# Attention with a memory, mixed with an S4 convolution, on one core: another stored order of the same 1,802 steps

## The chip, the core and the metric

The kernel runs on 1 core of one Trainium2 chip. The metric is device time in microseconds of one execution. The engines are named as in the profile: PE (TensorE) multiplies matrices, DVE (VectorE) and ACT (ScalarE) do the elementwise work, POOL (GpSimd) does next to nothing here, and SP (SyncE) issues all the DMA transfers.

## The reference

The input x has 2048 tokens of width 512. Two branches are computed from it and mixed per token:

```python
g = sigmoid((x * gate_w).sum(-1))            # one gate per token
out = g * A(x) + (1 - g) * B(x)

# A: 32 heads of width 16, tokens in 4 segments of 512
for s in range(4):
    a_dot = softmax(qs @ ks.T / 4 + causal_mask) @ vs      # inside the segment
    a_mem = (phi(qs) @ M) / (phi(qs) @ z + 1e-6)           # from the segments before
    o[s]  = sigmoid(beta) * a_mem + (1 - sigmoid(beta)) * a_dot
    M, z  = M + phi(ks).T @ vs, z + phi(ks).sum()          # phi(t) = t + 1 if t > 0 else exp(t)
A = o @ wo

# B: a long convolution per channel, 512 channels, 128 states
K[d, l] = Re( sum_n C[d,n] * exp(dt[d] * A[d,n] * l) * dt[d] * B[d,n] )
B = irfft(rfft(x padded) * rfft(K padded)) + x * Dskip
```

## The kernel before

The work is cut into 1,802 small steps, each an instruction or a short run of instructions on one engine, or one DMA transfer. They carry names:

- `pk`, `pq`, `tok` (s, hg): projections of segment s and group hg of 8 heads to keys, queries and values. Each is 4 matmuls and an eviction from PSUM.
- `sc`, `mk`, `pv`, `nrm` (s, hg, kind): scores, an exponential of 128x2048 on ACT (line 1067), a mask on DVE (line 1079) for the later groups, the product with the values and its division (lines 1041 and 1042). There are 80 such exponentials.
- `st`, `mem`, `os`, `oT`: the memory state, its use, the sum of both parts (line 1130) and the transposed heads.
- `pow` and `pwc` (h, k): the powers of the convolution's decay by squaring, for two halves h of the channels. Each power is copied into a second place by a DMA from SBUF to SBUF of 64 KB. `tab` (c): products of the powers (lines 1180, 1183 and 1187 on DVE) into tables for each of 4 quarters of the channels; `lag` (c): the convolution kernel from the tables.
- `xl1`: the first level of a Fourier transform of x, written to a scratch tensor in DRAM, `scr_Z`.
- For each half (a, b) of the channels and t from 0 to 15: `Zx`, `CT`, `CD` load a piece of `scr_Z` and of the constants `c_DNM` (128x768 and 128x1280); `X` is the second level of the transform, whose result is copied to the other half of the partitions by two DMAs of 64 KB; `K` transforms the convolution kernel; `Y` (line 1298 on DVE) multiplies both, and `V` transforms back and is written by a DMA to where `fir` collects it.
- `fir`, `Cl`, `fin`: the last level with the token gate, out to DRAM and back, and the output projection with the gated add (lines 1365, 1368 and 1369).
- `gate`: the factors from beta (lines 857 to 863); `xTl`: x loaded and transposed (line 700 for segments 1 to 3).

Nothing in these steps is tied to a place in the program. A string, `ORDER`, lists all of them in one order; `build_kernel` reads it, and `replay` gives each engine its steps in that order. A word of the string is the step's number, then `a` or `v` where the step is an eviction that either ACT or DVE may do, then, after slashes, the number of the buffer for each tile that is taken there:

```python
        for w in ORDER.split():
            w = w.split("/")
            order.append((int(w[0].rstrip("av")), "ACT" if w[0][-1] == "a" else "DVE", [int(v) for v in w[1:]]))
        S.replay(order)
        S.emit()
```

So the string decides four things: the order on each engine and on SP's queue, which of ACT and DVE evicts, which buffer and which PSUM bank a tile gets, and with these what each instruction waits for. `emit` puts the waits in. An engine runs its steps strictly in its order: a step that waits holds up all behind it, and a DMA whose data is not ready holds up the transfers behind it on SP.

Of the kernel before, what the change touches and what calls it, by code (L numbers as in the profile page):

```python
# [369 lines left out]
15/0 8/1 0/0 9/4 25/6/0 14/0 26v 31/0/0 57/0 32 41/0 34/1 42/5 1202/1 6/0 10/0 35/2 33/10 36/3 60/5 37 38 39 40/3 58/7 61v/0 47/0 43/11 23/0 11/1 48/1  # L370
16/0 49/4 51/0 50 59a 44 1220/5/0 64/7 12/2 62/3 45 1218/0 1219a 63 3/0 1210/3/1 18/0 1/0 65v/8 74/2 46 76/0 1221a 75 27/1/1 204/0/2 22/0 201/2/1/0
28v 53/0 88/6 13/3 20/0 86/1 87 1211a 195/0 29/1/0 77v/5 176/1 100/2 52/11 19 98/0 4/0 99 205a 209/0/0 56/0 1222 54/2 30v 202a 203 110/3 112/3 66
220/0/0 17 111 67 113v/1 221 181/4 89v/0 182/0 192/0 124/0 122/1 123 101v/7 125v/2 222 179/3 102 1223/0 213/1 207/2 210a 126 778/0 114 136/2 177/1 90
229/0/1 134/2 1208/3 137v/4 103 214v 230 249/0/0/1 215/1/1/0 55 208a 231 135 196 115 1209a 240/0/2 178/0 180 91 24/0 241 250a 197/0 146/2 216 78 148/3
1236/3/0 252/0/1 147 1237a 70/1 184/1 1212 211/2 242 161v/3 206 982v/0 217 253a 1226/3/1 986 1234/1 224/0/3 149v/6 198/0 79 987/1 68/2 251 988 978v/0
979v 254/0/0/1 212a 980v 1235a 225 127 7/0 293/2/0 981v 162 223/1 160/4 69 226 236/0/0 379/1 158/2 163 294a 993/0 255 992 138 183 159 237 994 218 227
228 232 290/2/2/0 170v/9 256 150 1238 999/0 1224/0 983 984/1 233/0 998 171 1227a 238 985 139 1205/3/0 1225a 291a 270/0/3 271 1206a 235/2 219/0/0
1203/3 234/0 370/0 989 272 257 1000 1228 1204a 80/0 82/6 239 151 995 261/0/1 1001 262 263 172 243 996/0 244 5/0 1002/1 258 1239/1/1 245/2 1241/3 997
292 193 265/0/2 246 1240a 1207 1004 266 1005/0 1229/1/0 1231/2 1242a 264/3 267 1243 277/0/1 194 259/0 278 185 1006 1003 1213/0/1 1232a 1230a 329/1/1/2
279 1214a 281/0/0 330a 1215/2 1244/0 282 990/0 1013 1233 268 269 1216a 991 283 81 276/0 1250/1/0 273 1007 332/2/1 1014/1 1008/0 304/0/3 333a 1015 305  # L380
1009 1016 1251a 280 1017/0 306 1217 1260/1/1 1011/1 284 1262/2 1261a 285 286/3 300/0/0 274/0 301 1010 1263a 1265/1 1018 371/1/0/1 302 334/2/0/0 335
316/0/2 1012 317 372a 92/2 275/1 1023/1/0 1019/3 1024 287 1020 1021 336 1025 94/0 318 93 1264 104/0 337 1027/0 1028 1022v 309/0/1 310 1036a/0 1038v/0
331 1266/2/1 1042 1026a 1043/1 106/2 1267a 107v/0 1268/3 1034v 311 386/1 1044 105 303/2 1269v 1049/0 116/2 307 308 1048 71v/1 312 1037v 1029a 315/3
320/0/0 321 1050 387a 313/1 1055/0 1040/1 247/0 1035a 2/0 322 1252/1 1039 314/0 1270 319 1278/2/1 341/0/1 117/0 342 323 1253a 324 118 1279a 248v/0 343
1254 1041 95v/5 1276/0 374/2/0 83v/7 1054 350/0/0 72 1277a 1045 325/3 295/1/1/1 128/0 73 351 96 1056 326 344/0 1052/1 375a 288/3 352 1245/2/0 345/0/2
346 1057 296 289v 1280 119v/2 1246a 1051 1247/3 429/2/2 347 129/1 130 297 568/0 373 361/0/1 1053 1046/0 362 140/0 430a 1248a 142/2 1058/1 348 141
1257/1/1 349 1255/2 353 382/3 363 1258a 1060 357/0/2 358 356/1 1047 354/0 1061/0 108 383a 120 359 384/3 393/0/0 1059 1062 394 97 1256a 1249 154/3 84
385a 1070/1 355/1 1069 1281/0/0 395 380/2 360 298 1064/0 364 381a 1071 397/0/2 1063 1259 398 131v/3 1072 1067/1 1282a 399 1066 299/0 1283/2 1271/3/1
132 1284a 1272a 409/0/3 1033/0 1068 109 410 1273/2 426/3/1/0 1065 1073/1 365 1030 366/0 1031 85 1032 338 411 413/0/1 414 1074 1285 1274a 367 427a
152/0 396/2 1079/3/0 428 1075/1 1287/0 1076 1077 339 1286/1 415 1080 153 143v/4 1275 1083/0 1084 578/0 155v/6 1081 199 1092v/0 402/0/0 1078a 1090v  # L390
1299/0 186/1 121 1300/1 400 403 166/0 1085a 187/0 1096/0 1091v 1082a 474/0/2/1 133 164/3 156 1093v 1094v/0 1314/1 401 165 1099/1 1301/0 1098 1095 404
523/1/1 457/0/2 458 1088 1100 524v 167a/8 368/3 405 168 1087 144 173v/9 408/1 475a 459 412 1302/0/0 1097 416 417 441/0/0 1288/2 1089 369v 442 406/0
1105/0 1102/1 418/1 388/3/0/0 200 376/0 1303a 1086 407/1 434/0/1/1 1306/2/1 443 1104 419 445/0/1 435 1307a 1106 174 169 1289/1/1 1290a 1101 1111/0 446
1110 436 627/2/0/2 1305 1293/0/0 447 260 437 1112 389 1103 327/1 1304 1294a 450/0/3 145 451 1292 1340/0 378/0 1108/0 444/0 1308/1 1291 328a 1313/0 452
157 390 1309/1/0 1113 1310a 628a 1107 1295/0 175 477/3/0 1312/0 448 476 449 1114/1 1119 461/0/0 462 1296/1/1 520/2/1/0 478a 1339/1 1315/3/0 1109
1327/2 1325/1 340 463 1316a 1297a 453 503/0/1 1116 504 1311/0 1317 1117/0 391 521a 1318 377 505 1345/3/1 454/2 456/1 1118 455/0 1319/2/0 1115 496/0/3
1328/0/2 1346a 497 1320a 460 1329a 464 1366/1 1125 420/1/0/0 1326/1 1321/0 498 1126/1 1365/0 1322/0/0 433/0 1330 421 1323a 1338/0 1120/0 422 1127 423
507/0/2 508 1332/0/0 509 1122 465 392/2/1 431/1 1331 502/3 1298 1128 506 1379/2 1121 1352/1 1341/7/0 1353/0 438 1333a 1129/1 1334/0 1342a 1344 572/4/2
424/7 510 432 511 1343 482/0/1/0 573a 1123/0 1335/4/1 425a/0 1351/1 581/5 512/0 1130 1336a 468/3/1/0 585/4 1124 513/1 582a 1135/5/0 439 574/0 479/1
469 1136 1139/3 586a 1347/0 1140 470 522 483 1131/2 1137 1132 1133 471 1146v/0 1141a 1354/3/1 1149v 1138a 1324 487/0/0 484 1148v 466/0 1150v/0 1134a  # L400
488 1348/2/0 1358/0/1 1147a 1355a 1364/0 576/0 489 1152/1 1371/3/0 491/0/1 629 1151 1349a 467 1153 1357 1154 492 1155/1 1157 485 569/1/2/1 1359a 1372a
472/0 1356 1367/2/0 528/3/0/1 1391/1 493 1156 535/0/2 481/1 1163 1160 1161/0 570v 536 1162 490/1 1368a 494 1360/1 1337 529 537 473a 480 530 579/2
1378/0 1167/0 495 571 1350 1164/1 1361/3/1 499 1166 544/0/0 580a 1369 545 1362a 1370 1377/1 500/0 1168 501 1397/0/1 514/1/5/0 1144 1373/1 1405/0
1392/1 1374/1/0 546 1398a 539/0/1 1390/0 540 1375a 1169 1380/0/0 630/1/0 515 525/1 1381a 1165 516 1404/1 1384/0/0 517 538/2 1418/2 531 541 1393/3/1
1385a 1175 1383 551/0/2 1158/1 1172 1159 1173/0 1382 1376 1176/1 1394a 552 542 486/0 636/3/1/0 543 1363 553 547 1386/0 532 555/0/1 556 631a 1387/1/0
# [1055 lines left out]
```

## Time and profile before

| | us |
|---|---|
| median of 3 runs | 287.19 (286.94 to 290.25) |
| profiled execution | 287.07 |
| its span | 285.3 |
| DVE busy | 265.6 (93%) |
| ACT busy | 261.4 (92%) |
| PE busy | 248.9 (87%) |

The span runs from the first to the last instruction; the execution's own time holds 1.8 us around it. A row of the profile names the engine, the line, the operation, the tensors by name, and at its end in brackets the idle time ahead of it on its engine, with what ended that. Most PSUM evictions pass through one helper, so they carry its lines 226 (ACT) and 227 (DVE); matmuls carry line 663 and plain DMAs line 222.

### The profile page before, as it was taken

The numbers are of one execution on the slowest core, as the hardware profiler recorded it, in microseconds if no ns is written. First come the engines' busy times: TensorE is split into PE (matmuls) and PEld (weight loads), VectorE is DVE, ScalarE is ACT, GpSimd is POOL, SyncE is SP. The second block draws the span as 40 slices with busy tenths as digits, with TensorE's granted clock in tenths as the row PEclk, the third lists the DMA queues.
The fourth block names the chain that finished last, engine by engine and source line by source line (L and its number), as shares of the span: only waits on it lengthen the run. The fifth ranks groups of instructions, "written<-read, shape, count | busy, mean of one in ns | idle before, by whom it ended". The sixth has DMA issues, their size and how long they took to land.

```text
span 285.3 us, 9041 instructions
## 1 busy us (share of the span) xinstructions
PE 248.9 (87%) x3741; PEld 170.4 (60%) x3776; DVE 265.6 (93%) x634; ACT 261.4 (92%) x314; POOL 5.9 (2%) x9
## 2 busy tenths in 40 slices
PE   2767778788687999999999899999989999999995
PEld 1423444465344756777767477876766676889552
DVE  1999999999999999999999999996889999999795
ACT  2999999999999999989999999999878999998832
POOL 0003100000001000000001000000000000000000
PEclk9999997999999999999999999999999999999999
DMA  6969364402825727653656576787667876356966
GB/s 179 212 209 169 97 155 149 149 7 84 122 88 169 181 58 208 186 165 87 177 174 194 137 219 181 194 242 200 192 199 210 258 209 190 77 146 175 264 175 203
DMA packets 61211, 47.71 MB, mean 167 GB/s; under 512 B 23921, under 2 KB 57074, under 8 KB 61170
## 3 DMA queue, kind: packets, MB, share of 16 engines
q1 hardware_dynamic: 61170, 47.13, 60.1%
q8 instruction: 30, 0.49, 0.8%
q14 instruction: 11, 0.09, 0.1%
HBM read 26.79 MB, written 8.39 MB: 123 GB/s over the span
## 4 chain that ended last, share of the span: by engine, by line
PE 35%; DVE 33%; ACT 26%; issue 2%; DMA 2%; SPq 0%; DVEq 0%
PE psum L663 34%; ACT sb L1067 16%; ACT sb L226 8%; DVE sb L1180 5%; DVE sb L1187 5%; DVE sb L1183 5%; DVE sb L227 3%; DVE sb L794 2%; DVE sb L787 2%; DVE sb L786 2%; DMA sb<-sb 1%; DVE sb L1042 1%; DMA sb<-in_B_A_im_dram 1%; ACT sb L940 1%; DVE sb L795 1%
## 5 line engine op out<-in xcount | busy, mean ns | idle before, releaser
L663 PE MATMUL psum<-sb 128*128 128x17 bf16 (+12 forms) x3605 | 241.3, 231 | 26.8 <-ACT sb L1067 14.3
L663 PEld LDWEIGHTS psum<-sb 128*128 128x128 bf16 (+4 forms) x3640 | 161.3, 99 | 100.9 <-ACT sb L1067 27.5
L1067 ACT ACTIVATE sb<-psum 128x2048 bf16<-128x2048 f32 x80 | 152.1, 1901 | 4.7 <-PE psum L663 3.8
L226 ACT ACTIVATE sb<-psum 128x512 bf16<-128x512 f32 (+4 forms) x154 | 88.4, 628 | 3.2 <-PE psum L663 2.8
L1180 DVE TENSOR_TENSOR sb<-sb 128x512 bf16<-128x512 bf16 (+3 forms) x48 | 33.0, 697 | 0.0
L1187 DVE TENSOR_TENSOR sb<-sb 128x512 bf16<-128x512 bf16 (+3 forms) x48 | 32.1, 681 | 0.0
L1183 DVE TENSOR_TENSOR sb<-sb 128x512 bf16<-128x512 bf16 (+3 forms) x48 | 31.9, 674 | 0.0
L227 DVE CAST sb<-psum 128x512 bf16<-128x512 f32 (+2 forms) x41 | 27.6, 674 | 3.0 <-PE psum L663 2.8
L1079 DVE TENSOR_TENSOR sb<-sb 128x1024 bf16<-128x1024 bf16 (+1 forms) x40 | 22.4, 569 | 1.3 <-ACT sb L1067 1.2
L1298 DVE TENSOR_TENSOR sb<-sb 128x1024 bf16<-128x1024 bf16 x32 | 21.7, 680 | 1.9 <-DMA sb<-sb 1.8
L1042 DVE TENSOR_TENSOR sb<-psum,sb 128x256 bf16<-128x256 f32 x32 | 13.2, 414 | 0.1
L227 DVE COPY sb<-psum 128x512 bf16<-128x512 bf16 (+2 forms) x15 | 7.2, 480 | 5.7 <-PE psum L730 5.3
L785 ACT ACTIVATE sb<-sb 128x512 f32<-128x512 f32 x18 | 11.8, 656 | 0.0
L1368 ACT ACTIVATE sb<-psum,sb 128x512 bf16<-128x512 f32 x8 | 5.2, 689 | 5.7 <-DMA out_dram<-sb 5.5
L1041 DVE RECIPROCAL sb<-psum 128x16 f32<-128x16 f32 x32 | 7.9, 248 | 1.4 <-PE psum L663 1.3
L912 POOL COPY sb<-sb 128x128 bf16<-128x128 bf16 x4 | 5.5, 1462 | 149.1 <-PE psum L663 124.0
L1121 DVE TENSOR_TENSOR sb<-psum,sb 128x512 bf16<-128x512 f32 x12 | 8.2, 684 | 0.1
L794 DVE CAST sb<-sb 128x512 bf16<-128x512 f32 x19 | 8.0, 434 | 0.0
L996 ACT ACTIVATE sb<-sb 128x512 bf16<-128x512 bf16 x12 | 7.5, 636 | 0.1
L940 ACT ACTIVATE sb<-psum 128x512 bf16<-128x512 bf16 x12 | 7.6, 637 | 0.0
L1337 DVE TENSOR_TENSOR sb<-psum,sb 128x512 bf16<-128x512 f32 x11 | 7.4, 687 | 0.2 <-PE psum L663 0.2
L786 DVE TENSOR_TENSOR sb<-sb 128x256 f32<-128x256 f32 x18 | 7.5, 417 | 0.0
(74 smaller groups left out, 120.7 us busy)
## 6 DMA issues: line engine op xcount, KB each, us to landing
sb<-c_DNM SPq DMA_DIRECT2D x28, 320.0 KB, 3.8
sb<-sb SPq DMA_DIRECT2D x84, 64.0 KB, 2.9
sb<-c_DNM SPq DMA_DIRECT2D x28, 192.0 KB, 3.1
scr_Z<-sb SPq DMA_DIRECT2D x16, 256.0 KB, 2.2
sb<-scr_Z SPq DMA_DIRECT2D x32, 128.0 KB, 3.1
sb<-sb SPq DMA_DIRECT2D x32, 128.0 KB
sb<-in_A_x_dram SPq DMA_DIRECT2D x5, 512.0 KB, 4.8
scr_C<-sb SPq DMA_DIRECT2D x8, 256.0 KB, 2.6
```

Of the source, the lines that this page charges most:

```text
L226: fa = lambda e: e.activation(dst(), src(), ACT.Copy)
L227: fd = lambda e: e.tensor_copy(dst(), src())
L663: mm = lambda e, o_, l, r_, st, sp, **kw: e.matmul(o_, lhsT=l, rhs=r_, start=st, stop=sp, skip_group_check=True, **kw)
L786: op("DVE", ("V1", 256), lambda e, nz=nz, sq=sq: e.tensor_tensor(ap(nz, 0, n=256), ap(sq, 0, n=256), ap(sq, 256, n=256), ALU.subtract), r= ...
L794: "DVE": (("Vs2", 512), lambda e, dst=dst, src=src: e.tensor_copy(dst(), src()))})
L1042: op("DVE", ("V1", 256), lambda e: e.tensor_tensor(ap(o1, gi * 16, [[128, 4], [32, 4], [1, 16]]), ap(T, dims=[[68, 4], [17, 4], [1, 16]]), ...
L1067: o = op("ACT", ("Ax", 2048), lambda e, P=P, pT=pT: e.activation(ap(pT, n=2048), ap(P, n=2048), ACT.Exp, scale=0.25), r=[P], w=[pT])
L1079: op("DVE", ("V2", 128 * nb), lambda e, pT=pT, dims=dims: e.tensor_tensor(ap(pT, dims=dims + [[1, 128]]), ap(pT, dims=dims + [[1, 128]]), ...
L1180: op("DVE", ("V2" if n > 1 else "V1", 256 * n), lambda e: e.tensor_tensor(run(tile, ne, dst, 1), run(tile, ne, src, sstep), fac(cl * 512), ...
L1183: op("DVE", ("V2" if n > 1 else "V1", 256 * n), lambda e: e.tensor_tensor(run(t2, n, 0, 1), run(tile, ne, src, sstep), fac(cl * 512 + 256) ...
L1187: op("DVE", ("V2" if n > 1 else "V1", 256 * n), lambda e: e.tensor_tensor(D_(), D_(), ap(t2, n * 128, [[-n * 128, 2], [2 * n, 64], [1, 2 * ...
L1298: op("DVE", ("V2", 1024), lambda e, Y=Y, XAB=XAB, K3=K3: e.tensor_tensor(ap(Y, dims=[[512, 2], [1, 512]]), ap(XAB, dims=[[512, 2], [1, 512 ...
```

## The change

The string `ORDER` is replaced by another one. The steps, the buffers' sizes and places, the constants and all other code are the same. It was found by a search whose model lets a DMA's landing depend on the packets in which TensorE's instructions are fetched. 42 evictions and copies change engine: 22 go from DVE to ACT and 20 from ACT to DVE. Between them the counts on DVE go from 634 to 632 steps. Every one of the 70 lines of the string changes; the first of them reads

```diff
@@ -367,76 +367,76 @@
 ORDER = """
-15/0 8/1 0/0 9/4 25/6/0 14/0 26v 31/0/0 57/0 32 41/0 34/1 42/5 1202/1 6/0 10/0 35/2 33/10 36/3 60/5 37 38 39 40/3 58/7 61v/0 47/0 43/11 23/0 11/1 48/1
...
+8/3 0/0 15/0 9/0 14/0 23/0 25/0/2 57/1 192/0 26v 1202/0 195/4 31/1/0 193 32 196 6/0 1/0 41/13 34/11 3/0 33/0 36/1 60/0 37 42/2 58/5 38 11/3 10/0 197/0
...
```

What that moves is shown by the instructions as they stand on an engine. On DVE the program begins with the eviction of the first parameters (line 227) and the decay's steps (lines 751 to 757). Before, its first rows were

```order
L227 COPY sb<-psum 128x1024
L752 TENSOR_TENSOR sb<-sb 128x256 x2
L751 TENSOR_TENSOR sb<-sb 128x256
L754 TENSOR_SCALAR sb<-sb 128x256
L755 TENSOR_SCALAR sb<-sb 128x256
```

and now they are

```order
L227 COPY sb<-psum 128x1024
L861 TENSOR_SCALAR sb<-sb 128x32
L858 TENSOR_SCALAR sb<-sb 128x32
L752 TENSOR_TENSOR sb<-sb 128x256 x2
L751 TENSOR_TENSOR sb<-sb 128x256
L754 TENSOR_SCALAR sb<-sb 128x256
L755 TENSOR_SCALAR sb<-sb 128x256
```

Two of the gate's steps (lines 858 and 861) have come in behind the first eviction; on ACT two others (lines 857 and 862) stand likewise around its first exponential, and the load of beta they need is SP's fifth transfer, where it was the ninth.

On SP the load of the constants for step Xb5 is the row `c_DNM 128x768`. Before, it stood behind a load for K (`128x1280`) and the copies of Xb3 and Xa15:

```order
L222 DMA sb<-scr_Z 128x512
L222 DMA sb<-sb 64x512 x2
L222 DMA sb<-c_DNM 128x1280
L222 DMA sb<-sb 64x512 x2
L222 DMA sb<-c_DNM 128x768
```

and now it stands behind a write of V (`8x16x512`) and one copy:

```order
L222 DMA sb<-scr_Z 128x512
L222 DMA sb<-sb 64x512
L222 DMA sb<-sb 8x16x512
L222 DMA sb<-c_DNM 128x768
L222 DMA sb<-sb 64x512
```

It has moved from the 207th to the 200th of SP's 301 transfers.

138 lines of the change are left out of this document (69 added, 69 removed).

## The prediction

> **What bounds the kernel now.** I read the page's busy shares first, then the busy time by stage, then the chain, and last the waits. The page's first part:
>
> ```profile
> PE 248.9 (87%) x3741; PEld 170.4 (60%) x3776; DVE 265.6 (93%) x634; ACT 261.4 (92%) x314; POOL 5.9 (2%) x9
> ```
>
> Three engines are busy for about nine tenths of a span of 285.3 us, so no order of the same steps can be shorter than DVE's 265.6 us plus what cannot be filled at both ends. The stages show where the rest lies (columns: stretch, its length, then busy us and instructions of PE, weight loads, DVE, ACT and POOL, granted clock, DMA share, GB/s):
>
> ```profile
> 0.00:5.30 5.30, 1.09 (x9) 0.87 (x9) 0.02 (x1) 1.28 (x1) 0.40 (x5) 1.00 0.49 127
> 5.30:100.00 94.70, 73.42 (x1129) 43.26 (x1141) 93.98 (x243) 92.94 (x121) 4.73 (x3) 0.98 0.57 141
> 100.00:190.00 90.00, 85.15 (x1376) 62.98 (x1385) 88.53 (x201) 87.70 (x111) 0.73 (x1) 1.00 0.60 169
> 190.00:278.00 88.00, 84.94 (x1218) 61.55 (x1228) 78.83 (x186) 77.51 (x80) 0.00 (x0) 1.00 0.67 193
> 278.00:285.30 7.30, 4.29 (x20) 1.70 (x18) 4.19 (x9) 1.98 (x3) 0.00 (x0) 1.00 0.61 200
> ```
>
> Up to 190 us DVE and ACT are full: DVE idles 0.72 us, then 1.47 us, ACT 1.76 and 2.30 us. From 190 to 278 us TensorE is the full one (idle 3.06 us) while DVE idles 9.17 us and ACT 10.49 us. A stall counts on DVE and ACT in the first 190 us and on TensorE after that. The chain that ended last agrees at its end (start, length, what):
>
> ```profile
> 239.06 17.98 PE psum L663 x281
> 257.28 6.54 PE psum L663 x92
> ...
> 277.97 2.60 PE psum L663 x12
> 280.60 0.70 ACT sb L1368
> 281.66 1.42 DVE sb L1365 x2
> ```
>
> TensorE carries most of the last 40 us, and one copy with two gated adds closes it.
>
> **The change part by part.** All 1,802 steps stay, so the sum has terms only for waits that go, waits that come, and work that changes engine. It is made against the profiled execution, 287.07 us (its span of 285.3 us and 1.8 us around it), 0.12 us under the median of 287.19.
>
> *A, the load for step Xb5.* At 208 us all three engines stand:
>
> ```profile
> 202.76 0.58 SPq L222 DMA_DIRECT2D sb<-c_DNM  x1
> DMA to landing us min/median/max: 5.3/5.3/5.3
> 206.80 0.69 DVE L1079 TENSOR_TENSOR sb<-sb 128x1024 bf16<-128x1024 bf16 x1
> 208.14 2.62 PE L663 MATMUL psum<-sb 128*128 128x256 bf16 x34 [1.26 <-DVE sb L1079]
> 208.56 0.69 DVE L227 CAST sb<-psum 128x512 bf16<-128x512 f32 x1 [1.07 <-PE psum L663]
> 210.16 0.60 ACT L226 ACTIVATE sb<-psum 128x512 bf16<-128x512 f32 x1 [1.35 <-PE psum L663]
> ```
>
> The view names L1079 of DVE, but that ended at 207.49, 0.65 us before TensorE went on, and Xb5 does not read it. What Xb5 reads is the load issued at 202.76: with 5.3 us to land it arrives at 208.06. On SP's queue this load is the `c_DNM 128x768` row. Before, from the write of Vb12 (`8x16x512 x2`, its second) on:
>
> ```order
> L222 DMA sb<-sb 8x16x512 x2
> L222 DMA sb<-scr_Z 128x512
> L222 DMA sb<-sb 64x512 x2
> L222 DMA sb<-c_DNM 128x1280
> L222 DMA sb<-sb 64x512 x2
> L222 DMA sb<-c_DNM 128x768
> ```
>
> and now, from the same write on:
>
> ```order
> L222 DMA sb<-sb 8x16x512
> L222 DMA sb<-scr_Z 128x512
> L222 DMA sb<-sb 64x512
> L222 DMA sb<-sb 8x16x512
> L222 DMA sb<-c_DNM 128x768
> ```
>
> Six transfers stood between, now three, and the load has gone from the 207th to the 200th of SP's 301 transfers; Xb5 keeps its place on TensorE. Three issues of about 0.6 us are 1.8 us, over the 1.26 us wanted. What is late next is TensorE's own work before it, which ended at 206.88. I take **-1.2 us** (0 to -1.35). In the stretch of that load lies one packet of TensorE's instructions:
>
> ```profile
> q8 instruction: 1, 0.02, 1.1%
> ```
>
> The Trainium skill (Runtime: NRT & Kernel Launch, Instruction fetch mechanics) says that an engine's instructions are refilled in blocks of 16 KiB by a DMA queue of its own and that crossing a block is mostly hidden. The 0.02 MB row agrees with the block; by that rule alone nothing is gained from dodging packets and A would come from the earlier issue only, which is one of the rivals' cases below.
>
> *B, the product Yb14.* In the three DVE waits for copies (1.8 us in all) this is the large one:
>
> ```profile
> DVE sb L1298 <- DMA sb<-sb: 1.8, 3, 1.1
> 193.82 0.69 DVE L1298 TENSOR_TENSOR sb<-sb 128x1024 bf16<-128x1024 bf16 x1 [1.13 <-DMA sb<-sb]
> ```
>
> Its last copy is now 16 places ahead of it in the list instead of 10. But it lies in the stage where TensorE is full, so of 1.13 us I count **-0.2** (0 to -1.1).
>
> *C, the end.* The copy of the last transposed heads (step oT3.3) moves ahead of one gated add of 0.75 us, and the sum feeding it no longer queues behind four adds. TensorE runs through there without a gap (2.60 us from 277.97), so the copy is covered: **-0.2** (+0.3 to -0.8, that one add).
>
> *D, work that changes engine.* Of the steps that ran before 190 us, nine go from DVE to ACT and ten the other way. Their prices on DVE (mean ns of one is the last number ahead of the idle part):
>
> ```profile
> L227 DVE CAST sb<-psum 128x512 bf16<-128x512 f32 x38 | 25.8, 681 | 2.7 <-PE psum L663 2.5
> L227 DVE CAST sb<-psum 128x480 bf16<-128x480 f32 x2 | 1.3, 648 | 0.0
> L227 DVE COPY sb<-sb 128x256 bf16<-128x256 bf16 x17 | 3.9, 287 | 0.1
> ```
>
> Five full evictions come (Ka9, Va8, tok2.2, Ka14, Kb14) and three go (Xa9, pk2.2, pq2.2), +1.36; two evictions of table 1's lags come, at most 1.3; one copy of 0.29 more goes than comes, and two casts of the powers go, priced as two of the larger copies at some 0.4 each; the two transposed-head copies cancel. That is +1.3 us on DVE, which idles 2.2 us in that time. After 190 us thirteen steps leave DVE and ten come, where it has room. I take **+0.5** (-0.7 to +1.3).
>
> *E, the gate steps.* They sat in full stretches:
>
> ```profile
> 4.65 0.50 SPq L222 DMA_DIRECT2D sb<-in_A_beta_dram  x1
> 14.48 0.18 DVE L861 TENSOR_SCALAR sb<-sb 128x32 f32<-128x32 bf16 x1
> 18.48 0.23 ACT L857 ACTIVATE sb<-sb 128x32 f32<-128x32 bf16 x1
> 24.12 0.25 ACT L862 ACTIVATE sb<-sb 128x32 f32<-128x32 f32 x1
> ```
>
> Now they run in the first 7 us, where ACT stands until 5.82 us, and beta's load is issued fifth instead of ninth, one issue (0.5 us) ahead of x. That frees some 0.3 us on DVE and 0.5 on ACT, and ACT's first step now waits for beta. Issued near 2.7 us and landing by 5.4, it is hidden behind the wait for the first matmuls; should it take as long as the x loads beside it,
>
> ```profile
> sb<-in_A_x_dram SPq DMA_DIRECT2D x2, 512.0 KB, 4.6
> ```
>
> it lands at 7.3 and everything starts 1.5 us late. **-0.3** (-0.6 to +1.5).
>
> *F, waits that come.* The product Ya9 waited a little before:
>
> ```profile
> 154.75 0.68 DVE L227 CAST sb<-psum 128x512 bf16<-128x512 f32 x1
> sb<-sb SPq DMA_DIRECT2D x2, 64.0 KB, 3.3
> 159.11 0.69 DVE L1298 TENSOR_TENSOR sb<-sb 128x1024 bf16<-128x1024 bf16 x1 [0.36 <-DMA sb<-sb]
> ```
>
> On DVE, before, from that CAST (Xa9) to Ya9 (L1298):
>
> ```order
> L227 CAST sb<-psum 128x512
> L1183 TENSOR_TENSOR sb<-sb 128x512
> L1041 RECIPROCAL sb<-psum 128x16
> L1187 TENSOR_TENSOR sb<-sb 128x128x16
> L970 TENSOR_TENSOR sb<-sb 128x272
> L1187 TENSOR_TENSOR sb<-sb 128x128x4
> L1180 TENSOR_TENSOR sb<-sb 128x128x4
> L227 CAST sb<-psum 128x512
> L1298 TENSOR_TENSOR sb<-sb 128x1024
> ```
>
> and now, where Xa9 is copied by ACT about beside the first of these rows:
>
> ```order
> L1187 TENSOR_TENSOR sb<-sb 128x128x4
> L227 CAST sb<-psum 128x32x16
> L1183 TENSOR_TENSOR sb<-sb 128x512
> L1079 TENSOR_TENSOR sb<-sb 128x4x128
> L1298 TENSOR_TENSOR sb<-sb 128x1024
> ```
>
> Seven instructions and 3.7 us lay between; now four, about 1.9 us at 0.4 to 0.7 each, against copies that need 3.3 us and a second issue. Ya9 may stand for up to 2 us, with DVE's table steps and TensorE's Va9 behind it. DVE may also run late against ACT there, which would hide it. **+0.6** (0 to +2.0).
>
> The sum is -1.2 - 0.2 - 0.2 + 0.5 - 0.3 + 0.6 = -0.8 us, so **286.3 us**. With all low ends it is 287.07 - 4.55 = 282.5, with all high ends 287.07 + 5.1 = 292.2.
>
> **The rivals.** *The waits only move.* In so full a queue the earlier load lands as late, or Xb5's wait reappears at another load: A and B are 0, the sum is +0.6, about 287.7. For it speaks that SP's queue still holds the same 301 transfers at a DMA share of 0.67; against it that A's load is ahead of three whole transfers.
>
> *Much more is gained.* TensorE's waits for ACT's exponentials shrink:
>
> ```profile
> PE psum L663 <- ACT sb L1067: 14.3, 27, 1.5
> ```
>
> Were every idle microsecond of TensorE between 100 and 278 us (4.85 + 3.06) to go but 2, and E and C to give their low ends, the time would be 287.07 - 5.9 - 1.4 = 279.8; half way there is 283. Against it: most of the 14.3 us lies before 100 us, where TensorE is not the bound, and TensorE's list after 100 us is the old one with shifts of a few places, so no TensorE work moves out of the full stage.
>
> *Slower: the transposing loads hold SP ahead of the table's copies.* One such load occupies SP for up to 4 us:
>
> ```profile
> 19.37 3.98 SPq L700 DMA_TRANSPOSE sb<-in_A_x_dram  x1
> 23.41 1.97 SPq L222 DMA_DIRECT2D sb<-sb  x3
> ...
> 27.21 1.28 SPq L222 DMA_DIRECT2D sb<-sb  x2
> ...
> 33.70 1.88 SPq L700 DMA_TRANSPOSE sb<-in_A_x_dram  x1
> 39.07 1.82 DVE L1180 TENSOR_TENSOR sb<-sb 128x1024 bf16<-128x1024 bf16 x2
> ```
>
> SP's rows (`128x2x128` are the copies of the powers) before, from the first copy to the second transposing load:
>
> ```order
> L222 DMA sb<-sb 128x2x128
> L222 DMA sb<-in_A_x_dram 128x2048
> L700 DMA_TRANSPOSE sb<-in_A_x_dram 128x4x512
> L222 DMA sb<-sb 128x2x128 x3
> L222 DMA sb<-in_B_Dskip_dram 128x4x1
> L222 DMA scr_Z<-sb 128x2x512
> L222 DMA sb<-sb 128x2x128 x2
> L222 DMA sb<-c_G 128x256
> L222 DMA sb<-sb 128x2x128
> ```
>
> and now, from the second copy on:
>
> ```order
> L222 DMA sb<-sb 128x2x128 x2
> L222 DMA sb<-in_B_Dskip_dram 128x4x1
> L222 DMA sb<-sb 128x2x128 x3
> L700 DMA_TRANSPOSE sb<-in_A_x_dram 128x4x512
> L222 DMA scr_Z<-sb 128x2x512
> L222 DMA sb<-sb 128x2x128 x2
> L222 DMA scr_Z<-sb 128x2x512
> L222 DMA sb<-sb 128x2x128
> L700 DMA_TRANSPOSE sb<-in_A_x_dram 128x4x512
> ```
>
> Six copies are now ahead of the hold and three behind it, the last of them feeding the table step that ran at 39.07 and now stands 5 places earlier, near 37.3 us. If the hold begins near 27 us (before, the sixth copy's issue ended at 28.5, behind the first hold), it ends at 31, five issues of 0.6 us follow, and a copy of 3 us lands by 37: nothing is lost. The point from which it decides is a start of the hold past 28 us; at 31 us the copy lands at 41, DVE stands 3.5 us in a stage where it has no room, and the next hold does the like for the last copy, some 2.5 us: 287.07 + 6 = **293**.
>
> **How the numbers follow.** Forecast 286.3: 0.5. Only moved, 287.7: 0.25. Much gained, 280 to 283: 0.13. Slower, 293: 0.12. A measurement here tells some 2% (281.4 and 292.9) from no change. Half of the gaining case lies under 281.4, so faster gets 0.08 with its edge; of the slower case five sixths lie over 292.9, so slower gets 0.10; same 0.82. The range reaches from the sum of all low ends, 282.5, to 291.5, a little under that of all high ends, which will not all meet, and leaves out under 2 in 10.
>
> **What would show it.** A is right if no TensorE wait over 1 us is left near Xb5; B if the waits of L1298 for `sb<-sb` fall under 1.8 us; F if one of them sits at Ya9 near 156 us; E if ACT's first activation starts by 6 us; the slower rival if DVE waits for `sb<-sb` at a table line (L1180 to L1187) near 37 us. I am wrong if the first 190 us end by more than 3 us earlier or later with TensorE's list unchanged, since no term reaches that.

## The result, and the profile after

| us | before | after |
|---|---|---|
| median of the comparison | 287.06 | 290.33 |
| profiled execution | 287.07 | 291.39 |
| its span | 285.3 | 289.6 |

The ratio is 1.0106, 95% interval 1.0061 to 1.0151: the new order is slower by 1.1%, some 3 us, where 0.8 us less was forecast. The same kernel timed again (run 7 below) gave 1.0172 (1.0127 to 1.0218). The time lies inside the range given, on the wrong side of the old one. The median of after counts an execution of 295.15 us at a mean clock of 0.976, which the ratio leaves out.

The page of after: the engines' busy time has hardly moved (DVE 264.5 for 265.6, ACT 261.9 for 261.4), so the loss is idle time.

```profile
PE 252.8 (87%) x3776; PEld 171.6 (59%) x3776; DVE 264.5 (91%) x632; ACT 261.9 (90%) x314; POOL 4.6 (2%) x9
```

By stage (the columns as before: PE, weight loads, DVE, ACT, POOL, clock, DMA share, GB/s):

```profile
5.30:100.00 94.70, 72.73 (x1101) 42.42 (x1100) 91.46 (x232) 91.53 (x122) 2.56 (x3) 0.98 0.52 140
100.00:190.00 90.00, 85.88 (x1387) 61.87 (x1384) 86.95 (x200) 86.07 (x104) 1.61 (x1) 0.98 0.56 156
190.00:278.00 88.00, 85.19 (x1237) 62.67 (x1235) 78.02 (x185) 80.28 (x85) 0.00 (x0) 1.00 0.71 204
```

DVE now idles 3.24 us up to 100 us (0.72 before) and 3.05 us up to 190 (1.47 before): 4.1 us more in the two stretches where it is the full engine. TensorE idles 2.81 us in its own stretch, 0.25 less than before. The rows of the list of waits that bear on this, longest first, say for whom (total us, times, longest):

```profile
PE psum L663 <- DMA sb<-c_DNM: 2.6, 4, 1.0
DVE sb L1183 <- DMA sb<-sb: 1.7, 1, 1.7
ACT L762 <- DVE sb L757: 1.4, 1, 1.4
DVE sb L1369 <- DMA sb<-scr_C: 1.3, 1, 1.3
DVE sb L754 <- ACT sb L764: 1.1, 1, 1.1
DVE sb L1298 <- DMA sb<-sb: 0.3, 1, 0.3
```

The waits of the products (L1298) are down from 1.8 to 0.3 us; in their place stand waits for pieces of `c_DNM`, for a copy at a table line, and two at the head, at lines 757 to 764, which before did not have.

Both orders run the 80 exponentials (L1067) in the same sequence, so the start of the n-th in one trace less that in the other is how far after lags there. The last column is the same for a second profile of after, that of run 7, against the same profile of before:

| n-th of L1067 | before | after | lag | lag in run 7 |
|---|---|---|---|---|
| 21 | 83.04 | 83.98 | 0.94 | 0.91 |
| 27 | 101.43 | 102.66 | 1.23 | 0.34 |
| 28 | 104.64 | 106.94 | 2.30 | 0.34 |
| 49 | 175.59 | 177.54 | 1.95 | 0.43 |
| 54 | 194.42 | 198.69 | 4.27 | 1.39 |
| 59 | 210.65 | 213.39 | 2.74 | 0.10 |
| 80 | 270.09 | 273.64 | 3.55 | 2.57 |

About 0.95 us stands at 47 us and from 65 to 83 us; 1.1 come between 102.7 and 106.9 us and some 2.3 between 178 and 197 us; 1.3 are won back near 208 us, where Xb5's wait was; 0.8 are lost again by 253 us. The 1.1 us are not a landing's: TensorE's granted clock is low there (columns as above), and ACT waits 0.94 us for TensorE in it. The wait of 1.66 us at 97.9 us (below) takes the lag from 0.39 to 1.20 us, after it had fallen to that from 1.30 at 93 us.

```profile
102.00:106.00 4.00, 3.97 (x32) 2.55 (x32) 4.00 (x16) 3.06 (x5) 0.00 (x0) 0.57 0.25 51
```

Run 7's profile, at a mean clock of 0.998, took 290.45 us and has its loss elsewhere: it has caught up with before by 210 us, and loses 1.0 us at a load (Kb2, 211 us), 1.5 us at the copy below and 0.8 us behind the last exponential.

```profile
255.11 0.69 DVE L227 CAST sb<-psum 128x512 bf16<-128x512 f32 x1 [1.59 <-DMA sb<-sb]
```

Only the head's lag stands in both alike, up to 96 us. The head and the landings are looked at in turn.

**The head.** ACT's table load for the sine (L762) in before, then in after, then DVE's wait in after:

```profile
6.90 0.75 ACT L753 ACTIVATE sb<-sb 128x256 f32<-128x256 f32 x2 [0.49 <-DVE sb L752]
7.74 1.28 ACT L762 ACT_TABLE_LOAD   x1
9.03 0.42 ACT L762 ACTIVATE sb<-sb 128x256 f32<-128x256 f32 x1
```

```profile
7.11 0.75 ACT L753 ACTIVATE sb<-sb 128x256 f32<-128x256 f32 x2 [0.37 <-DVE sb L752]
9.28 1.28 ACT L762 ACT_TABLE_LOAD   x1 [1.41 <-DVE sb L757]
10.57 0.42 ACT L762 ACTIVATE sb<-sb 128x256 f32<-128x256 f32 x1
11.33 0.29 DVE L754 TENSOR_SCALAR sb<-sb 128x256 f32<-128x256 f32 x1 [1.11 <-ACT sb L764]
```

The sine needs two things: DVE's L757, and ACT's own work before it. Before, the load of 1.28 us ran while ACT waited for L757; after, it waits for L757 itself and runs behind it, and DVE stands 1.11 us for what follows. The instructions with their waits show why. The sine's step has two waits. The activation carries one of them, and the other holds the table load in front (in the traces it is an instruction of line 330 directly ahead of the load). `q_ACT` and `q_DVE` are the signals of the two engines. Before:

```
L762 ACT_TABLE_LOAD [waits q_ACT]
L762 ACTIVATE sb<-sb 128x256 [waits q_DVE]
```

and after:

```
L762 ACT_TABLE_LOAD [waits q_DVE]
L762 ACTIVATE sb<-sb 128x256 [waits q_ACT]
```

`emit` sorts an instruction's waits by the place of what it waits for in the string. Step 35 (ACT's own work, no neighbour of it changed) stands ahead of DVE's steps 38 and 39 in the old string and behind them in the new one, and that alone swaps the two.

**The landings.** Three transfers of after that were waited for: the copy pwc1.4 (issued at 92.5 us), the loads CDa14 (172.3) and CDa15 (189.9). Who waited, then for each the time to landing, then the row of TensorE's instruction packets between issue and landing:

```profile
97.93 0.43 DVE L1183 TENSOR_TENSOR sb<-sb 128x512 bf16<-128x512 bf16 x1 [1.66 <-DMA sb<-sb]
178.48 1.67 PE L663 MATMUL psum<-sb 128*128 128x256 bf16 x19 [1.00 <-DMA sb<-c_DNM]
196.40 1.28 PE L663 MATMUL psum<-sb 128*128 128x256 bf16 x10 [1.01 <-DMA sb<-c_DNM]
```

```profile
DMA to landing us min/median/max: 5.3/5.3/5.3
DMA to landing us min/median/max: 6.1/6.1/6.1
DMA to landing us min/median/max: 6.4/6.4/6.4
```

```profile
q8 instruction: 1, 0.02, 2.5%
q8 instruction: 1, 0.02, 1.0%
q8 instruction: 1, 0.02, 1.9%
```

The medians on the page are 2.5 us for such a copy and 3.8 us for such a load. In each of the three flights one packet of TensorE's instructions is fetched, as in the flight of CTb5 in before. Over all of SP's transfers issued after 30 us (268 in before, 271 in after; issue and last landing of each from the trace), those with such a packet in flight take 3.78 us on average in before (126 of them) and those without 2.72; in after 3.80 (120) and 2.80. So a packet goes with 1.0 us more. A long flight also meets a packet more easily: with the packets' times shifted at random against the transfers, the same sum still gives 0.4 us in before and 0.5 in after. Some 0.5 to 0.7 us are left beside a packet, and this is no proof of a cause.

### The profile page after: what moved, and what is told of

It is laid out like the page before. It is cut to its first block, busy times and chain, and to the rows that moved or that the text cites. A ratio compares the mean times of both kernels' runs of the same rounds, so it can differ in the third digit from the quotient of the medians.

```text
span 289.6 us, 9062 instructions
## 1 busy us (share of the span) xinstructions
PE 252.8 (87%) x3776; PEld 171.6 (59%) x3776; DVE 264.5 (91%) x632; ACT 261.9 (90%) x314; POOL 4.6 (2%) x9
## 4 chain that ended last, share of the span: by engine, by line
DVE 30%; PE 27%; ACT 19%; DMA 15%; SPq 5%; issue 4%; DVEq 0%; ACTq 0%
PE psum L663 26%; ACT sb L1067 10%; ACT sb L226 7%; DMA sb<-sb 6%; DVE sb L1180 5%; SPq L222 5%; DVE sb L1183 5%; DVE sb L1187 4%; DMA sb<-c_DNM 4%; DMA sb<-scr_C 3%; DVE sb L786 2%; DVE sb L227 2%; DVE sb L787 2%; DVE sb L794 2%; DMA sb<-in_A_beta_dram 1%
## 5 line engine op out<-in xcount | busy, mean ns | idle before, releaser
L663 PE MATMUL psum<-sb 128*128 128x17 bf16 (+12 forms) x3640 | 246.0, 232 | 25.7 <-ACT sb L1067 15.8
L663 PEld LDWEIGHTS psum<-sb 128*128 128x128 bf16 (+4 forms) x3640 | 162.0, 99 | 103.2 <-ACT sb L1067 28.1
L1067 ACT ACTIVATE sb<-psum 128x2048 bf16<-128x2048 f32 x80 | 151.9, 1899 | 3.7 <-PE psum L663 3.2
L226 ACT ACTIVATE sb<-psum 128x512 bf16<-128x512 f32 (+2 forms) x155 | 88.3, 624 | 6.2 <-PE psum L663 5.3
L1180 DVE TENSOR_TENSOR sb<-sb 128x512 bf16<-128x512 bf16 (+3 forms) x48 | 32.7, 696 | 0.0
L227 DVE CAST sb<-psum 128x512 bf16<-128x512 f32 (+2 forms) x39 | 26.0, 670 | 2.4 <-PE psum L663 2.1
L1298 DVE TENSOR_TENSOR sb<-sb 128x1024 bf16<-128x1024 bf16 x32 | 21.7, 684 | 0.5 <-DMA sb<-sb 0.3
L227 DVE COPY sb<-psum 128x512 bf16<-128x512 bf16 (+2 forms) x16 | 7.6, 473 | 7.5 <-PE psum L730 5.3
L1337 DVE TENSOR_TENSOR sb<-psum,sb 128x512 bf16<-128x512 f32 x13 | 8.8, 680 | 0.3 <-PE psum L663 0.2
L1121 DVE TENSOR_TENSOR sb<-psum,sb 128x512 bf16<-128x512 f32 x12 | 8.2, 685 | 0.1
L787 DVE SCALAR_TENSOR_TENSOR sb<-sb 128x256 f32<-128x256 f32 x18 | 7.5, 416 | 0.0
L794 DVE CAST sb<-sb 128x512 bf16<-128x512 f32 x17 | 7.0, 412 | 0.0
```

Source lines behind the costliest of these rows:

```text
L226: fa = lambda e: e.activation(dst(), src(), ACT.Copy)
L227: fd = lambda e: e.tensor_copy(dst(), src())
L663: mm = lambda e, o_, l, r_, st, sp, **kw: e.matmul(o_, lhsT=l, rhs=r_, start=st, stop=sp, skip_group_check=True, **kw)
L787: op("DVE", ("V1", 256), lambda e, nz=nz, Z=Z: e.scalar_tensor_tensor(ap(nz, 256, n=256), ap(Z, 0, n=256), 2.0, ap(Z, 256, n=256), ALU.mul ...
L1067: o = op("ACT", ("Ax", 2048), lambda e, P=P, pT=pT: e.activation(ap(pT, n=2048), ap(P, n=2048), ACT.Exp, scale=0.25), r=[P], w=[pT])
L1180: op("DVE", ("V2" if n > 1 else "V1", 256 * n), lambda e: e.tensor_tensor(run(tile, ne, dst, 1), run(tile, ne, src, sstep), fac(cl * 512), ...
```

## The experiments

Fifteen kernels other than the two were built from words of the strings, or from a few matmuls put ahead; "before" is run beside each. In the diffs a word is a step's number with its buffers.

**1. The early gate in the order of before.** Steps 23, 192, 193, 195, 196, 197 go to after's places:

```diff
-... 9/4 25/6/0 14/0 26v 31/0/0 57/0 32 41/0 ...
+... 9/4 25/6/0 14/0 23/0 192/0 26v 195/0 193 31/0/0 57/0 32 196 41/0 ...
```

> The order of before, with only the gate's steps and the load of beta put where the changed order has them (beta 5th of SP's transfers, ahead of x; lines 857, 862 first on ACT, 861, 858, 863 among DVE's first steps). Theory (the head is worth what the two traces show from 36 to 83 us): the first transposes of x start 0.8 us later, at 7.5 us, and the time rises by 0.7 to 1.0 us, ratio near 1.003. Rival (term E of the prediction): nothing to 0.5 us less, ratio 0.998 to 1.000, since the steps fill idle time of ACT and DVE in the head and free 0.9 us of DVE and ACT later.

Measured: 1.0084 (1.0051 to 1.0118), some 2.4 us; in its profile the lag is 1.0 to 1.3 us from 47 us to 190 us. The theory's sign holds, its reason is part of it: x's first transposition begins at 7.22 us for 6.66, and ACT is 0.65 us late by 17.2 us. At the first L1067 it is 1.67 us late, and this further 1.0 us comes from a table load. In before ACT has a table load at the gate's exponential, and in this run it is gone from there:

```profile
17.18 1.28 ACT L857 ACT_TABLE_LOAD   x1
18.48 0.23 ACT L857 ACTIVATE sb<-sb 128x32 f32<-128x32 bf16 x1
18.61 0.61 ACT L785 ACTIVATE sb<-sb 128x512 f32<-128x512 f32 x1
```

```profile
18.86 0.63 ACT L785 ACTIVATE sb<-sb 128x512 f32<-128x512 f32 x1 [1.04 <-DVE sb L786]
19.51 1.28 ACT L1067 ACT_TABLE_LOAD   x1
20.80 1.88 ACT L1067 ACTIVATE sb<-psum 128x2048 bf16<-128x2048 f32 x1
```

The gate's exponential had carried the table load into the time in which ACT would have waited for DVE; taken away, ACT waits 1.04 us and loads behind the wait. This part is the head's loss again at another place: 1.28 us hidden by a wait or exposed behind it.

**2. The changed order with the gate late.** The reverse move; the steps taken out go behind 10, 87 and 231 and ahead of 222, 206 and 194, and step 195 takes buffer 0 for 4:

```diff
-... 14/0 23/0 25/0/2 57/1 192/0 26v 1202/0 195/4 31/1/0 193 32 196 6/0 ...
+... 14/0 25/0/2 57/1 26v 1202/0 31/1/0 32 6/0 ...
```

> The changed order, with only the gate's steps and the load of beta put back to about where before has them. TensorE's instructions are the same, so its packets stay where they are. Theory (loss in the head): 0.7 to 1.0 us less than the changed kernel, about 289.2 where that gives 290; the three late landings at 98, 178 and 196 us stay. Rival (the loss is the new order of DVE's and ACT's work as a whole): within 0.3 us of the changed kernel.

Measured: 1.0156 (1.0110 to 1.0203). Nothing is won: the table load for the sine still waits 1.41 us for L757 in its profile, and DVE 1.20 us for L764. In the changed order the gate's place is not what costs.

**3. CTb5 alone (term A).**

```diff
-... 704 1545/2 1528/1/0 1563 1487 757/5 684 1583/4 966 ...
+... 704 1545/2 1528/1/0 1583/4 1563 1487 757/5 684 966 ...
```

> The order of before, with only the load CTb5 put three transfers of SP earlier, ahead of the copies of Xb3 and Xa15 (206th to 204th place, issue near 201.6 us in place of 202.8). Theory (term A of the prediction, a gain that lasts to the end): it lands near 204 us, ahead of the packet of TensorE's instructions at 205.8 us, the 1.35 us wait at Xb5 goes, and the time falls by 1.0 to 1.3 us, ratio near 0.996. Rival (waits only move): the landings behind it take the wait's place and the time stays within 0.3 us.

Measured: 0.9997 (0.9970 to 1.0025). Its profile has the load at the 205th place, issued at 201.43 us and landed at 205.19, and no wait at Xb5; it runs 1.49 us ahead of before's from 211 us to the end, and that execution took 285.6 us. The timed runs show none of it: at most 0.3%, 0.9 us. One profiled execution said 1.5 us, and twelve timed ones said nothing.

**4. The changed order with its packets shifted.** 48 small matmuls in front of TensorE's first step, while it stands idle:

```diff
+ if e == "PE": eng.wait_ge(*tok(self.prog["POOL"][0])); self.pad(eng)
+ S.pad = lambda e, P=P: [mm(e, ap(P, n=8), ap(onerT, n=128, np_=1), ap(onerT, n=8, np_=1), True, True) for _ in range(48)]
```

> The changed order, word for word, with 48 small matmuls of 8 columns (96 instructions of TensorE, 6 KB) ahead of TensorE's first step, where TensorE stands idle to 4.2 us. Every later packet of TensorE's instructions is then fetched 96 instructions, some 3.6 us, earlier; nothing else changes. Theory (the new waits are landings that share their flight with a packet): the waits for pwc1.4 near 98 us, CDa14 near 178 us and CDa15 near 196 us go, 2 to 3 us together; other transfers meet packets and take back some, so 286.5 to 289 us. Rival (the waits come from SP's order and the bytes in flight, not from the packets): the three waits stay at 0.7 us or more each and the time is within 0.4 us of the changed kernel.

Measured: 1.0207 (1.0162 to 1.0251). The waits at pwc1.4 and CDa14 are gone from its profile, CDa15's is 0.68 us, as the theory has it; yet it is slower. TensorE itself now stands (the run of matmuls that was cut, what came behind, and the total by the list of waits):

```profile
92.82 2.21 PE L663 MATMUL psum<-sb 128*64 128x40 bf16 x127
96.71 1.05 PE L663 MATMUL psum<-sb 128*64 128x40 bf16 x13 [1.68 <-issue]
PE psum L663 <- issue: 4.1, 8, 1.7
```

In after the last row reads `PE psum L663 <- issue: 0.2, 1, 0.2`. Between these two rows nothing is waited for that the profile shows; a packet of 1.1 us began at 94.1. The run of 127 matmuls of 40 columns takes 2.2 us, and with a weight load to each that is 254 instructions. The page has 30 packets for 3,776 matmuls and as many weight loads, some 250 to a packet: this run uses up a whole packet in 2.2 us. The Trainium skill (Runtime: NRT & Kernel Launch, Instruction fetch mechanics) has the crossing of a block mostly hidden; here nothing is seen of it in after, and in this run TensorE stands for 1.7 us. That the packet is the cause is read from its place: the profile names no releaser, and TensorE goes on 1.5 us behind the packet's end.

**5. The table load of the changed order ahead of its wait.** One word; no engine's order changes:

```diff
-... 58/5 38 11/3 10/0 197/0 39 35/3 47/1 ...
+... 58/5 35/3 38 11/3 10/0 197/0 39 47/1 ...
```

> The changed order with one word moved: step 35 (a step of ACT in the decay's preparation) stands ahead of step 38 (line 756 on DVE) in the string. No engine's and no queue's order changes by it; only the two waits ahead of ACT's sine change places: the wait for DVE's line 757 stands behind ACT's table load (line 762) as in before, in place of ahead of it. Theory (the steady 0.95 us of the stretch from 36 to 83 us comes from this table load being held): the load of 1.28 us runs while ACT waits, DVE's wait of 1.1 us at 11.3 us goes, and the time falls by 0.8 to 1.0 us against the changed kernel of the same call. Rival (it comes from the load of beta ahead of x): under 0.3 us.

Measured: 1.0088 (1.0055 to 1.0121), beside 1.0172 (1.0127 to 1.0218) of the changed kernel on the same chip: 0.8% less, more than the 1 us expected, though the intervals only just miss each other, and against the first measure of after (1.0106, 1.0061 to 1.0151) the gain is not clear of the noise. The load is back in the wait, and DVE's wait is gone:

```profile
7.84 1.28 ACT L762 ACT_TABLE_LOAD   x1
9.13 0.42 ACT L762 ACTIVATE sb<-sb 128x256 f32<-128x256 f32 x1
10.04 0.33 DVE L754 TENSOR_SCALAR sb<-sb 128x256 f32<-128x256 f32 x1
```

From 34 to 40 us this profile runs 1.25 us ahead of after's; behind that its clock was low and it is not compared.

**6. Three transfers of the changed order earlier.** Word by word:

```diff
-... 1074 339 85 426/1/0/0 ... 403 121 1094a/0 ...
+... 1074 339 121 85 426/1/0/0 ... 403 1094a/0 ...
-... 1443/0 1455/0 606/2 ... 644/0/1 1469/2 1427a ...
+... 1443/0 1469/2 1455/0 606/2 ... 644/0/1 1427a ...
-... 668 1441 658/0 ... 1532/0 1482/1 1522a ...
+... 668 1482/1 1441 658/0 ... 1532/0 1522a ...
```

> The changed order with three transfers of SP put earlier: the copy pwc1.4 five places (ahead of pwc1.1), the load CDa14 one place (ahead of CTa13), the load CDa15 two places (ahead of Va11's write). Theory (the late landings at 98, 178 and 196 us are worth their waits): PE's two waits of 1.0 us and DVE's of 1.7 us shrink to under 0.4 us each and the time falls by 2 to 3 us against the changed kernel of the same call. Rival (waits only move: other landings take their place, as in the shifted run): within 0.8 us, with new waits for other pieces of c_DNM or copies in the same stretches.

Measured: 1.0071 (1.0041 to 1.0101), 1.0% under the changed kernel beside it, some 2.9 us. In its profile the three waits are gone and the new ones are smaller (0.7 us at TensorE for a copy, 0.4 us for another at L1180). The theory holds in sign and in size against run 7; against the first measure of after, 1.0106, the gain is not clear of the noise. The clock is in it too: at a mean clock of 0.998 or more, the few executions left average 289.96 us for after (4), 288.69 for run 5 (4) and 288.67 here (3), so that each of the two edits is worth some 1.3 us there, less than the 3.7 us that the three waits add up to.

**7 and 8. Both kernels once more.**

> The changed kernel, word for word, once more, to be compared in one call and to see whether its waits come again. If the late landings belong to the order: PE waits 1.0 us for CDa14 near 178 us and for CDa15 near 196 us and DVE 1.7 us for pwc1.4 near 98 us again, within 0.3 us each, and 289 to 291 us. If they are chance of one execution: other waits stand there, and the head's 0.95 us alone comes again.

> The kernel before, word for word, once more, for a second profile. If its waits belong to the order: PE waits 1.26 us for CTb5 at 208 us and DVE 1.1 us for Yb14's copies at 194 us again. If they are chance: other waits, of about the same sum, and the gain of putting CTb5 earlier could not be seen in the times.

Measured for after: 1.0172, its profile 290.45 us. The head's two waits come again to 0.1 us. Of the landings CDa14 comes again (0.89 us) and pwc1.4 shrinks to 0.63, CDa15's is gone, and others stand at `c_DNM` for Kb2 (0.81) and at L227 for a copy (1.6 us). Before's second profile, one execution of 288.03 us, has 0.85 us for CTb5 and 0.67 us at Yb14, and 0.98 us at CTa14, which the first lacked, and 0.83 us at Ya9, where the first had 0.36 (for the two loads the view names another engine; which load it is follows from its landing, at 209.02 and 184.34 us). So the head's waits for another engine came alike in both profiles, and a wait for a landing is partly of one execution.

**9. The mended order.** Edits 5 and 6 together, and Cla0 and Cla3 behind Clb2 and Cla1 at the end:

```diff
-... 1737 1514/0 873v ... 934 1517/0 1740 1738 ... 1778 1515 1770/1/4 ...
+... 1737 873v ... 934 1740 1514/0 1738 ... 1778 1515 1517/0 1770/1/4 ...
```

> The changed order with what the two runs before it mended put together (the wait at the table load; pwc1.4, CDa14 and CDa15 earlier), and at the end the loads Cla0 and Cla3, which are needed last, behind Clb2. Theory (the loss is these waits, and they add up): about 1 us from the head, 2.5 to 3 us from the three landings and up to 1 us from the end, together 4 us below the changed kernel, 286 to 287.5 us, as before within 0.5%. Rival (waits only move): 289 us or more.

Measured: 1.0056 (1.0026 to 1.0086). Two thirds of the 1.72% of run 7 are gone, or half of the first measure's 1.06%, not all: the two edits alone took off 0.84% and 1.01%, and together, on another chip, they took off 1.2%.

**10. The order of before with seven transfers moved**, on SP alone; CTb5 as in 3, and

```diff
-... 562/1/0/1 1201 591 ... 1455/1 1449/1/1 ... 1459a 1544/3 654 1462/1/1 1468/4 1546/2 ...
+... 562/1/0/1 591 ... 1455/1 1201 1449/1/1 ... 1459a 1468/4 1544/3 654 1462/1/1 1546/2 ...
-... 1699 1702a 960/3 1532/1 669/0 ... 710 1700 748/0/2 ... 1474 1712/1/0 ...
+... 1699 1700 1702a 960/3 669/0 ... 710 748/0/2 ... 1474 1532/1 1712/1/0 ...
-... 937 1514/0 946/0/3 ... 938 1515/0 939/0 1759/1/3 1740 1739 1775 ...
+... 937 946/0/3 ... 938 939/0 1759/1/3 1740 1514/0 1739/0 1515 1775 ...
```

> The order of before with transfers of SP alone put in another order, each where a wait stood in one of its two profiles: CTb5 ahead of Xb3's copies, Xb14's second copy right behind its first, CDb1 behind Xa14's copies, CTa14 ahead of CTb2, a piece of lag3 behind CTa13, and at the end Cla0 and Cla1 behind Clb2 and Clb1. Theory (waits at landings are worth their sum, 2.5 to 3.5 us of them in the profiles): 1.5 to 3 us below before, ratio 0.990 to 0.995. Rival (waits only move, as CTb5's gain was lost): within 0.8 us of before.

Measured: 1.0008 (0.9985 to 1.0031). The waits for CTb5, CTa14 and Yb14 are gone from its profile, one of 0.74 us stands at Yb1 instead, and the time is that of before. Here the rival holds: waits only move.

**11. The shift by 48 in the order of before**, with the two lines of run 4.

> The order of before, word for word, with the same 48 small matmuls ahead of TensorE's first step, so that the packets of TensorE's instructions begin 96 instructions earlier. Theory (an order is fitted to where its packets fall): TensorE stands still inside a run of small matmuls (lag, 128x40, or st, 128x17) by 1 us or more where a packet now falls into it, other landings come late, and the time rises by 1 to 4 us, ratio 1.004 to 1.014. Rival (packets do not matter to this order): within 0.5 us.

Measured: 1.0106 (1.0065 to 1.0148). As in 4, TensorE stands behind the same kind of run:

```profile
93.83 1.00 PE L663 MATMUL psum<-sb 128*64 128x40 bf16 x32
96.56 2.77 PE L663 MATMUL psum<-sb 128*128 128x17 bf16 x20 [1.73 <-issue]
PE psum L663 <- issue: 2.3, 2, 1.7
```

and a load, CDa10, comes 1.9 us late. A packet began at 94.19 us and took 0.98, and TensorE goes on 1.4 us behind its end, as in 4. With this shift the order of before is as slow as the new one was unshifted.

**12. The table load behind its wait in the order of before.** One word again:

```diff
-... 10/0 35/2 33/10 36/3 60/5 37 38 39 40/3 ...
+... 10/0 33/10 36/3 60/5 37 38 39 35/2 40/3 ...
```

> The order of before with one word moved: step 35 stands behind step 39, so that ACT's table load at line 762 waits for DVE's line 757, as in the changed order. No engine's order changes. Theory: the 1.28 us load begins at 9.0 in place of 7.7 us, DVE waits about 1 us for ACT's line 764, and the time rises by 0.8 to 1.2 us, ratio 1.003 to 1.004. Rival (the head has slack and gives it back before 36 us): under 0.3 us.

Measured: 1.0075 (1.0044 to 1.0107), 1.3 to 3.1 us. In the profile ACT's load goes behind the wait, and DVE's wait comes, in two pieces:

```profile
9.08 1.28 ACT L762 ACT_TABLE_LOAD   x1 [1.41 <-DVE sb L757]
10.82 0.43 DVE L768 TENSOR_TENSOR sb<-sb 128x256 f32<-128x256 f32 x1 [0.69 <-ACT sb L762]
11.58 0.43 DVE L767 TENSOR_TENSOR sb<-sb 128x256 f32<-128x256 f32 x1 [0.33 <-ACT sb L765]
```

The lag is 1.1 us from 46 us to 112 us, then 1.4 to 1.6. With run 5 this shows the head's loss in both directions, without an instruction moved on any engine. The times (some 2 us) show more than the traces (1.0 to 1.6 us); why stays open.

**13 to 16. Small shifts of both orders**, with the lines of run 4 and

```diff
- for _ in range(48)]
+ for _ in range(16)]   # or 32
```

> The changed order, word for word, with 16 small matmuls (32 instructions of TensorE, 2 KB) ahead of TensorE's first step, so that its packets begin 32 instructions earlier. If the places of the packets carry the loss: a ratio to before that differs from the changed kernel's 1.011 to 1.017 by 0.005 or more, either way, with stalls of PE without a releaser or late landings elsewhere. If the order of the work carries it: 1.012 to 1.018 as without the shift.

> The same with 32 small matmuls (64 instructions). If the places of the packets carry the loss: a ratio that differs from the changed kernel's by 0.005 or more, and another one than with 16. If the order of the work carries it: 1.012 to 1.018.

> The order of before, word for word, with 16 small matmuls (32 instructions) ahead. If before owes its time to where its packets fall: slower by 1 to 3 us, ratio 1.004 to 1.010, as with 48. If a packet costs only where it falls into a run of small matmuls: within 0.003 of before, since the packet of 94.35 us then begins some 0.5 to 1 us earlier, near the start of the run at 92.4 us.

> The order of before with 32 small matmuls (64 instructions) ahead. If before owes its time to where its packets fall: slower by 1 to 3 us. If only a packet inside a run of small matmuls costs: within 0.003 of before unless the profile shows PE idle by 1 us or more without a releaser.

| matmuls ahead | before's order | after's order |
|---|---|---|
| 0 | 1 | 1.0106, 1.0172 |
| 16 | 1.0022 (0.9995 to 1.0050) | 1.0189 (1.0140 to 1.0238) |
| 32 | 1.0048 (1.0021 to 1.0074) | 1.0150 (1.0102 to 1.0198) |
| 48 | 1.0106 (1.0065 to 1.0148) | 1.0207 (1.0162 to 1.0251) |

After's order is about 1.0 to 1.7% slower than before's at each shift, and no shift brings it near. So the loss belongs to the order of the work, not to where the packets happen to fall in it; the packets' places are worth up to 1% on top, and no shift makes before's order faster. The added matmuls themselves are not the price: in before's order the first exponential starts at most 0.2 us later with them.

**17. The mended order with the gate late as well**: the edits of 9 and 2 together.

> The mended changed order (table load ahead of its wait, three transfers earlier, Cla0 and Cla3 last) with the gate's steps and the load of beta also put back to about where before has them. If the early gate costs in this order what it cost in before's (0.8 per cent there): 0.6 to 0.8 per cent below the mended order, ratio to before 0.998 to 1.001. If the head's loss in this order was the table load alone: the ratio stays at the mended order's 1.0056 within 0.002, since ACT stood idle for the same 1.3 us of a table load in either order.

Measured: 1.0112 (1.0071 to 1.0152). No gain, as the rival has it, but also no repeat of 1.0056 within 0.002; its profile has a 1.4 us wait for CDb6 and 1.4 us at Yb8. What the mended order still loses, 0.3 to 1.1%, stays open.

## Why the prediction was wrong, point by point

- **The step that failed is the list of waits that come.** The sum had terms "only for waits that go, waits that come, and work that changes engine", and for waits that come it held E's late beta and F's Ya9 alone. The wait at the sine's table load was in no term: the rows of ACT and DVE were read without their waits, which the new string swaps there. Runs 5 and 12 put it at 0.8%, some 2 us, both ways; the traces at 0.95 to 1.6. The landings that take the place of Xb5's wait were at nothing too; in after's profile three of them wait 3.7 us, and run 6 took 1.0% off.
- **E** gave -0.3 us and saw a cost only if beta landed late. Beta landed at 5.88 us and ACT's first activation began at 5.91, so the sign that was named for it did come; x's first transposition began at 7.49 for 6.66, but run 5 has it at 7.27 and is still 1.25 us ahead. In the order of before the early gate cost 0.84%, 2.4 us, for a high end of 1.5 (run 1); in the new order putting it back won nothing (run 2).
- **A** was right in the trace and not in the time. The wait at Xb5 is gone in after (no wait of TensorE over 1 us near it), and the lag falls by 1.3 us there: the load, now issued at 204.10 us, landed in 2.4 us for 5.3. But run 3, A alone, measured at most 0.9 us and 0.1 at the middle of its interval. It sized a wait for a landing from one execution.
- **Waits only move** was given 287.7, with the new waits as small as the old. That is where the second part of the loss lies: the waits moved to pwc1.4, CDa14 and CDa15 in one profile, to Kb2 and a copy in the other, and grew. The mechanism had a quarter of the chance, and its price was set too low, by up to the 1.0% that run 6 took off.
- **B** was right: L1298 waits 0.3 us for copies, for 1.8.
- **F** was not seen: no wait over 0.3 us stands at Ya9. With shifted packets a wait of 1.06 us did come at Ya9 (run 13), so the margin may have been as thin as computed.
- **C** failed in sign: from the transposition of the last heads (L1137, at 281.19 us, 277.58 before) to the end of the span it takes 8.4 us for 7.7, 0.7 more, with DVE waiting 0.62 and 0.65 us at two gated adds (L1369).
- **D** cannot be told apart: DVE's busy time fell by 1.1 us in all, where 1.3 more before 190 us was counted (its parts, 1.36 + 1.3 - 0.29 - 0.8, add up to 1.6).
- **The slower rival** named another place. DVE has no wait for a copy near 37 us; its wait at a table line is pwc1.4's at 97.9 us, where no transposing load holds SP.
- The bound given for being wrong, 3 us by 190 us, was just not reached: the lag there is 2.6 to 2.9 us. That the time still lies inside the range is luck: the high ends that reach it stand for a late beta, Ya9 and work on DVE, and none of these made the loss.

## What to carry to other kernels

Where an instruction has two waits, see which of them holds the table load ahead of it: here a load of 1.28 us was hidden while ACT waited, and held back by the wait it cost 1.0 to 1.6 us of the trace, with no instruction moved. The head's waits for another engine came alike in two profiles, but a wait for a landing has to be priced from several executions, since it moves from one to the next: taking such waits away won nothing in the order of before (runs 3 and 10) and 1.0% in the new one (run 6). An order can also depend on where TensorE's instruction packets fall in it: 96 instructions added in front cost the order of before 1.1%, 64 cost 0.5%, and 32 nothing clear.

## What the runs showed of the hardware that was not expected

- Transfers with a packet of TensorE's instructions in flight beside them took 3.8 us for 2.7 to 2.8, of which 0.5 to 0.7 us are more than chance meetings give. TensorE itself stood for 1.7 us where a packet fell beside a run of small matmuls (runs 4 and 11). Neither is shown to be caused by the packet.
- The granted clock went with the order. It was half of full speed for some 3 us near 22 us in the first profile of after:

```profile
21.00:23.00 2.00, 2.00 (x6) 0.63 (x5) 2.00 (x6) 2.00 (x2) 0.00 (x0) 0.50 0.34 111
```

  None of 99 executions of before had a mean clock under 0.993; of 71 of the changed order and its variants 37 were under 0.990, and of 74 of the variants of before 6. It does not carry the result: at a clock of 0.998 or more, 4 executions of after average 289.96 us and 71 of before 286.44. Leaving out run 15, whose clock was low throughout, the profiles have 20 stretches at half clock, of 3.4 us or two or three times that, and 18 of them begin where TensorE was busy for at most 67% of the 3.4 us ahead. From 15 to 20 us, ahead of the stretch above, TensorE has less to do in after (second row) than in before:

```profile
15.00:20.00 5.00, 3.64 (x26) 1.54 (x24) 5.00 (x13) 4.97 (x9) 0.00 (x0) 1.00 0.59 187
15.00:20.00 5.00, 2.44 (x24) 1.40 (x25) 5.00 (x14) 4.98 (x11) 0.00 (x0) 1.00 0.42 127
```

  Run 7's profile has the same gap (2.47 us busy of 5) and kept the full clock there, so TensorE's idle time goes with the low clock and is not shown to be all of its cause.
